# One token tile's down projection moved into the last twelve attention periods, and the first token sums loaded one at a time

## The chip, the cores and the metric

The kernel runs on one core of a Trainium2 chip. The metric is the device time of one execution in microseconds (us). Five engines work side by side, each through its own instructions in order: PE (matrix products), DVE (vector), ACT (activations), POOL (GpSimd) and SP, which here only issues DMA transfers; a transfer waits in SP's queue behind those issued ahead of it.

## The reference

32 heads of full attention (head width 16) beside a gated MLP, mixed by one gate per token; S = 2048 tokens, D = 512, F = 1792, all in fp32:

```python
def _A_ref(x, wqkv, wo):
    qkv = transpose((x @ wqkv).reshape(B, S, 3, H, Dh), 2, 0, 3, 1, 4)
    q, k, v = qkv[0], qkv[1], qkv[2]
    scores = einsum("bhqd,bhkd->bhqk", q, k) * Dh ** -0.5
    o = einsum("bhqk,bhkd->bhqd", softmax(scores), v)
    return transpose(o, 0, 2, 1, 3).reshape(B, S, D) @ wo

def _B_ref(x, w_gate, w_up, w_down):
    h = sigmoid(x @ w_gate) * (x @ w_up)
    return h @ w_down

g = sigmoid((x * gate_w).sum(-1, keepdims=True))
return g * _A_ref(x, wqkv, wo) + (1 - g) * _B_ref(x, w_gate, w_up, w_down)
```

## The kernel before

Every fp32 product is done as three products of operands split into a high and a low part (high by high, high by low, low by high); `split_weights` makes the two parts, by a cast and a subtraction.

After a start stage (values, first projections) come 256 *periods* (`NPER`), k = 0 to 255, and then an end stage. A period takes two steps of the attention: 8 score products (lines 574; "t" in the order strings) whose exponentials ACT computes (line 576), 8 products for row maxima (line 284, "m") that DVE reduces (line 286), and 32 small value products (line 715, `values(k)`). The maxima of a set are transposed and sent by SP through the DMA queue into rows of the query tile (`qs<-mt`, line 314) before the scores of that set are formed. Into every period 12 *half products* ("d0" on partitions 0 to 63, "d1" on 64 to 127) are woven, all into one bank of PSUM, `dn`. They come from a generator, `filling()`: first the projections of later heads' queries and keys (class `Sum`: both halves of a product add up in one bank; a run takes two periods), then the gate and up projections (class `Side`), for which sums and differences of token blocks ("token sums", `xm`) and of weights are formed on POOL. Two products on different halves of the partitions run side by side on PE; two on the same half one after another. Where both halves add up in one bank, PE may change halves only after an instruction of POOL that does nothing (`turn`), which waits for the last product and for which the next one waits.

PE's order in a period is a string written by hand (`STEADY`, and `LAST` for k = 248 to 255, where no row maxima are left). POOL's work is kept in a list, `later`, of which up to five pieces are run per period. The order of each engine's instructions is that in which the code issues them; the order of SP's queue is set by a scheduler. The gate and up results go to `gu_d` in DRAM. The token sums go to `xm_d` (line 335) and come back as tiles of four loads each (`mixed`, line 355).

The half-product work ends at k = 243. In periods 244 to 247 the strings still hold 12 slots, which stay empty. The first two weight tiles of the down projection, `wd0` and `wd1`, are split by POOL about k = 244; the others are loaded in pairs (`late_raw`, `late_next`), the first pair split at k = 252.

The end stage goes through 28 chunks, (c, f): c is a group of four token tiles, f a pair of rows of `w_down`. The hidden values of a chunk are loaded (`hidden_load`), gated by ACT and DVE and split (`hidden`, `hidden_split`); then come 6 products (line 919) for each of the four token tiles, into four banks. Between the chunks stand the heads' output products (`heads_out`, line 137): 8 pieces of 24 products. In all there are 672 down products and 192 of the heads.

Of the kernel before, what the change touches and what calls it, by code (L numbers as in the profile page):

```python
# [40 lines left out]
UPPER = FIRST + 4  # L41
EARLY = NPER - TAIL - 4
LOW, UP = 0, 1
MIX = ((((0, 0), "+", (1, 1)), ((0, 0), None, None)), (((0, 1), "-", (1, 1)), ((1, 0), "-", (0, 0))),
       (((0, 0), "+", (0, 1)), ((1, 0), "+", (1, 1))), (((1, 1), None, None), ((1, 1), None, None)))
BLOCKS = (((0, 0), (1, 0)), ((1, 1), (1, 1)), ((0, 0), (1, 1)), ((1, 0), (0, 1)), ((0, 0), (0, 0)), ((0, 1), (0, 1)))
# [3 lines left out]
def gated_mix(ctx, tc, x, xc, xmix, wqk, wv, wo, w_gu, w_down, gate_w, out):  # L50
# [25 lines left out]
    gu_d = dram.tile([2, NF, P, S], F32, name="gu_d")  # L76
    pv_d = dram.tile([NC, NPAIR, P, 256], F32, name="pv_d")
    rec_d = dram.tile([P, 512], F32, name="rec_d")

    warm = keep.tile([P, 96], F32, name="warm")  # L80
    dve.memset(warm, 0.0)
# [19 lines left out]
        lo.tensor_tensor(l, src, h.bitcast(F32), ALU.subtract)  # L101

    def raw_weights(src, shape, name, queue=sp):
        raw = keep.tile(shape, F32, name=name + "r", tag="wr", bufs=4)
        queue.dma_start(raw, src)
        return raw, shape, name

# [2 lines left out]

    def split_weights(loaded, *engines):
        raw, shape, name = loaded
        h = keep.tile(shape, F32R, name=name + "h", tag="wh", bufs=4)
        l = keep.tile(shape, F32R, name=name + "l", tag="wl", bufs=4)
# [44 lines left out]
    class Side:  # L159
# [12 lines left out]

        def done(self):
            return self.n == len(self.ops)

    def turn(*runs):

# [179 lines left out]

    parts = []

    def take(n):  # L360
        while parts and n:
            parts.pop(0)()
            n -= 1

    def mixtures():
        for cp in range(2):
            for fp in range(NF // 2):
                for a in range(2):
                    name = f"{cp}_{fp}_{a}"

                    def raw(n, rows=slice(0, P)):
                        t = keep.tile([P, 512], F32, name=f"r{n}_{name}", tag="wr", bufs=4)
                        sp.dma_start(t[rows, :], w_gu[a, fp, n, rows, :])
                        return t

                    def ready(n, x, y=None, op=None, rows=slice(0, P)):
                        h = keep.tile([P, 512], F32R, name=f"mh{n}_{name}", tag="wh", bufs=4)
                        l = keep.tile([P, 512], F32R, name=f"ml{n}_{name}", tag="wl", bufs=4)
# [49 lines left out]
        return arrive  # L428

    wd = []  # L430

    def filling():
        jobs = [(n, cp) for cp in range(2) for n in range(1, D // P)]
# [18 lines left out]
        for j, (n, cp) in enumerate(jobs):  # L452
            settle([raw for raw, _, _ in coming])
            ws, nxt = nxt, []
            for c in range(2):
                for i, w in enumerate(ws):
                    run = Sum(bankd(), unit(w, 2 * cp + c))
                    yield run
                    runs += 1
                    e = keep.tile([P, 512], F32R, name=f"qk{n}_{cp}_{c}_{i}", tag="er", bufs=6)  # L460
                    leave(e.bitcast(F32), run.o)
                    put_qk(e, (q_d, k_d)[i], n, 2 * cp + c)
                    next(mix, None)
# [12 lines left out]
        t = 0  # L476
# [1 line left out]
        for cp in range(2):  # L478
            for fp in range(NF // 2):
                for a in range(2):  # L480
                    arrive = combine(cp, fp, a)
                    order = [(j, g) for j in range(3) for g in ((LOW, UP) if a else (UP, LOW))] + [(3, LOW if a else UP)]
                    ws = []
                    for q, (j, g) in enumerate(order):
                        if len(ws) <= j:
                            ws.append(W.pop(0))
                        run = Side(bankd(), g, ws[j], T[j])
                        yield run
                        m = ((2, 1), (4, 3), (7, 6), (5, 5))[j][g]
# [12 lines left out]
                        take(1 if late_t and q < 4 and not cp else 2)  # L502
                if cp == 0 and fp == NF // 2 - 1:
                    late_t[3] = mixed(1, 3)
                    T = late_t
        arrived.pop(0)()
        wd.extend(split_weights(raw_weights(w_down[f * P:(f + 1) * P, :], [P, D], f"wd{f}")) for f in range(2))

    leave = lambda e, o: act.activation(e, o, AF.Copy)  # L509
    fill = filling()  # L510
# [116 lines left out]
    def down_late(f, raw, hi):  # L627
        if f < 6:
            for a in range(2):
                if f < 4:  # L630
                    h = keep.tile([P, D], F32R, name=f"wd{f + a}h", tag="wh", bufs=4)
                    l = keep.tile([P, D], F32R, name=f"wd{f + a}l", tag="wl", bufs=4)
                else:
                    h, l = wd45[:, a, 0, :], wd45[:, a, 1, :]
                split(h, l, raw[:, a, :], hi, pool)
                wd.append((h, l))
        else:
# [22 lines left out]
    def early_hidden(m, a):  # L660
        gu = loaded[m]
        dve.scalar_tensor_tensor(gu[:, 1, a], gu[:, 0, a], 1.0, gu[:, 1, a], op0=ALU.add, op1=ALU.mult)
        if a == 0:
            ready.append([[], []])
        h, l = [keep.tile([P, 512], F32R, name=f"h{i}_{m}_{a}", tag=("er", "wr")[m], bufs=(6, 4)[m]) for i in range(2)]
        split(h, l, gu[:, 1, a], dve, pool)
        ready[m][0].append(h)
        ready[m][1].append(l)
# [120 lines left out]
    stages = [[], []]  # L789
    for k in range(NPER):  # L790
        n = 2 * k
        if n + FIRST == NSTEP:
# [21 lines left out]
            pass  # L814
        elif run.done():
            run = next(fill, None)
        else:
            turn(run)
        work(3 if isinstance(run, Sum) and k % 2 else 4)
        urgent.extend(jobs)  # L820
        if 320 <= n < 448:
# [57 lines left out]
        split(oh, ol, ot, act, pool)  # L879
        return oh, ol  # L880

    bankt = turns([dn] + maxb)
    bankh = turns(banks)
    acc = {}

    def finish(t, o, gate):

# [4 lines left out]
        if (t, 0) in acc:  # L892
# [15 lines left out]
    heads = {}  # L908
    for n, (c, f) in enumerate(chunks):
        if f == 0:  # L910
            down = [bankt() for _ in range(4)]
# [71 lines left out]
```

## Time and profile before

| | us |
|---|---|
| time, median of three runs | 1692.49 (1691.63 to 1693.6) |
| the profiled execution, its own time | 1691.6 |
| its span, first to last instruction | 1689.8 |
| PE busy | 1681.1 |
| DVE busy | 1431.6 |
| ACT busy | 1335.4 |
| POOL busy | 1017.9 |

The profiled execution is 0.9 us faster than the median. Times in the rows of the profile count from the first instruction. A period of the loop is 5.52 us; the last value products of the periods start at 1489.27, and the end stage runs from there to the end. The granted TensorE clock is 0.999 on average.

### The profile page before, as it was taken

Reading aid. Unit: us, or ns where it says so; the run is one execution under the profiler, and the core shown is the slowest. Engines: PE = TensorE matmul, PEld = TensorE weight load, DVE = VectorE, ACT = ScalarE, POOL = GpSimd, SP = SyncE. Lnnn points to the kernel's source line nnn. Section 1 sums busy time; section 2 is a strip of 40 time slices with the busy share of each in tenths; the row PEclk is TensorE's granted clock in tenths of the full one; section 3 lists DMA queues with packets and bytes.
Section 4 is the critical chain, followed back from the end, with each engine's and each line's share of the span. In section 5 each row is a group of like instructions: output and inputs, shape, how many; then the busy total and the mean of one; then the engine's idle time right before and its main releaser. Section 6 shows DMA issues by size and latency. Waiting matters only on the chain.

```text
span 1689.8 us, 43420 instructions
## 1 busy us (share of the span) xinstructions
PE 1681.1 (99%) x16552; PEld 1153.2 (68%) x16552; DVE 1431.6 (85%) x2450; ACT 1335.4 (79%) x2668; POOL 1017.9 (60%) x1192
## 2 busy tenths in 40 slices
PE   9999999999999999999999999999999999999999
PEld 7866666666666666666666666666666666578887
DVE  6889989999999999999999999999999999567543
ACT  4188878888888888888888899999999988973321
POOL 1146655358878787776675777767777765452110
PEclk9999999999999999999999999999999999999999
DMA  9524675464444344442357242524242422176752
GB/s 259 116 83 167 181 250 144 125 162 135 127 136 139 120 145 126 120 121 79 89 154 209 84 114 80 130 71 120 83 116 78 107 83 95 61 266 224 243 194 72
DMA packets 125008, 228.54 MB, mean 135 GB/s; under 512 B 19008, under 2 KB 35648, under 8 KB 121792
## 3 DMA queue, kind: packets, MB, share of 16 engines
q1 hardware_dynamic: 124512, 225.24, 45.3%
q8 instruction: 131, 2.15, 0.6%
q14 instruction: 77, 0.63, 0.2%
q10 hardware_dynamic: 288, 0.52, 0.1%
HBM read 149.42 MB, written 75.76 MB: 133 GB/s over the span
## 4 chain that ended last, share of the span: by engine, by line
PE 98%; DMA 1%; ACT 1%; DVE 1%; SPq 0%; issue 0%; POOL 0%; ACTq 0%
PE dn L170 23%; PE sm L715 21%; PE sm L284 9%; PE st L284 9%; PE st L715 7%; PE sm L919 7%; PE dn L150 6%; PE sm L574 4%; PE st L137 4%; PE st L574 3%; PE dn L919 2%; PE st L150 1%; ACT p L576 0%; DMA xm<-xm_d 0%; DVE stat L286 0%; PE st L85 0%
## 5 line engine op out<-in xcount | busy, mean ns | idle before, releaser
L286 DVE TENSOR_REDUCE stat<-sm 128x1 f32<-128x512 f32 x1124 | 728.1, 682 | 77.3 <-PE sm L284 39.1
L576 ACT ACTIVATE p<-sm 128x512 f32<-128x512 f32 x1217 | 686.7, 630 | 7.5 <-PE sm L574 5.3
L286 DVE TENSOR_REDUCE stat<-st 128x1 f32<-128x512 f32 x924 | 606.7, 682 | 64.2 <-PE sm L574 27.0
L576 ACT ACTIVATE p<-st 128x512 f32<-128x512 f32 x831 | 499.6, 634 | 5.5 <-PE st L574 4.1
L170 PE MATMUL dn<-xm,mh 64*128 64x512 f32 x1568 | 485.6, 389 | 0.0
L574 PE MATMUL sm<-qs,ks 64*128 64x512 f32 x1217 | 445.5, 404 | 0.3 <-ACT p L576 0.2
L284 PE MATMUL sm<-ks,qs 48*128 48x512 f32 x1124 | 421.6, 421 | 0.4 <-ACT p L576 0.3
L284 PE MATMUL st<-ks,qs 48*128 48x512 f32 x924 | 367.9, 426 | 0.0
L715 PE MATMUL sm<-p,v 128*17 128x256 f32 x6080 | 365.1, 380 | 0.1
L574 PE MATMUL st<-qs,ks 64*128 64x512 f32 x831 | 325.7, 409 | 3.0 <-DMA qs<-mt 3.0
L170 PEld LDWEIGHTS dn<-xm,mh 64*128 64x128 f32 x1568 | 289.6, 185 | 29.7
L170 PE MATMUL dn<-xm,ml 64*128 64x512 f32 x784 | 304.0, 388 | 0.0
L715 PEld LDWEIGHTS sm<-p,v 128*17 128x17 f32 x6080 | 160.3, 97 | 169.4 <-ACT p L576 58.4
L284 PEld LDWEIGHTS sm<-ks,qs 48*128 48x128 f32 x1124 | 200.4, 185 | 87.6 <-DVE stat L286 76.5
L574 PEld LDWEIGHTS sm<-qs,ks 64*128 64x128 f32 x1217 | 219.1, 186 | 18.4 <-ACT p L576 3.1
L284 PEld LDWEIGHTS st<-ks,qs 48*128 48x128 f32 x924 | 167.0, 185 | 83.9 <-DVE stat L286 75.5
L733 POOL TENSOR_TENSOR sum<-sum,part 128x256 f32<-128x256 f32 x192 | 141.7, 738 | 86.9 <-ACT part L720 63.4
L407 POOL TENSOR_TENSOR m<-m,m 128x512 f32<-128x512 f32 x140 | 178.2, 1289 | 5.7 <-ACT m L509 5.7
L574 PEld LDWEIGHTS st<-qs,ks 64*128 64x128 f32 x831 | 152.7, 186 | 16.2 <-issue 4.6
L100 POOL CAST mxs<-mxs 128x4 fp32r<-128x4 f32 x128 | 24.1, 188 | 219.6 <-DVE mxs L298 219.3
L170 PEld LDWEIGHTS dn<-xm,ml 64*128 64x128 f32 x784 | 144.4, 184 | 11.8
L123 POOL TENSOR_TENSOR ml<-r,mh 128x512 fp32r<-128x512 f32 x112 | 144.0, 1286 | 7.0
(225 smaller groups left out, 2288.4 us busy)
## 6 DMA issues: line engine op xcount, KB each, us to landing
r<-in_w_gu_dram SPq DMA_DIRECT2D x112, 256.0 KB
gul<-gu_d SPq DMA_DIRECT2D x56, 512.0 KB
gu_d<-m SPq DMA_DIRECT2D x84, 256.0 KB
xm_d<-xm SPq DMA_DIRECT2D x32, 512.0 KB
xm<-xm_d SPq DMA_DIRECT2D x32, 512.0 KB
xm<-in_xmix_dram SPq DMA_DIRECT2D x24, 512.0 KB
qs<-q_d SPq DMA_DIRECT2D x90, 128.0 KB
ks<-k_d SPq DMA_DIRECT2D x90, 128.0 KB
```

The lines of the kernel that those rows point to most:

```text
L123: pool.tensor_tensor(l, src, h.bitcast(F32), ALU.subtract)
L137: pe.matmul(o, a, b, start=(i == 0), stop=(i == len(ops) - 1))
L150: mm = pe.matmul(self.o, a[rows], b[rows], start=(self.n == 0), stop=(self.n == 2 * len(self.ops) - 1))
L170: pe.matmul(self.o, a, b, start=(self.n == 0), stop=(self.n == len(self.ops) - 1))
L284: pe.matmul(t, qs[r:r + KM, qt * P:(qt + 1) * P], ks[r:r + KM, g * 512:(g + 1) * 512], start=True, stop=True)
L286: dve.tensor_reduce(stat[part][:, qt % 4, g:g + 1], t, axis=AX.X, op=ALU.max)
L407: pool.tensor_tensor(o, x, y, op)
L574: pe.matmul(o, ks[r:r + KR, (kt + a) * P:(kt + a + 1) * P], qs[r:r + KR, c * 512:(c + 1) * 512], start=True, stop=True)
L576: act.activation(pt[:, a, :], o, AF.Exp, scale=DH ** -0.5)
L715: pe.matmul(o[r:r + VW, :], v[:, 4 * k % 16 + a, h * VW:(h + 1) * VW], pts[b][:, a, 256 * i:256 * i + 256], start=(a == 0), stop=(a == 3))
L733: pool.tensor_tensor(s, s, e, ALU.add)
L919: pe.matmul(down[t], a, b, start=(f == 0 and m == 0), stop=(f == NF - 2 and m == 5))
```

## The change

Token tile 4 (`AHEAD`) leaves the end stage: its 42 products (14 rows of `w_down`, three each) are done as 84 half products, in the bank `dn`, in periods 244 to 255. Periods 244 to 247 take 12 each into slots that were empty; 248 to 251 take 18 upper halves and 252 to 255 18 lower halves, as the strings say. For this the hidden values of tile 4 are formed at k = 152 to 164 in four pieces (ACT, POOL, by `h_d` in DRAM), loaded again about k = 239 into a buffer of the token tiles, and all 14 tiles of `w_down` are loaded and split by POOL from k = 239 on; `wd0` to `wd3` stay for the end stage, the others are loaded a second time there, as before. The split weights have six buffers in place of four. The end stage makes 630 down products; the result of tile 4 is scaled out of `dn` by DVE at the fifth chunk and added with the heads.

The loads of the first two token sums are begun earlier (after runs 12 and 16, not 14 and 17), and each waits for ACT's copy of the run after which it is issued.

```diff
+    class Down(Sum):
+        def __init__(self):
+            self.o, self.n, self.last, self.token = dn, 0, None, None
+            self.ops, self.left = range(6 * NF // 2), [[], []]
+        def give(self, h, w):
+            for side in self.left:
+                side += terms([(h, w)])
...
-    def take(n):
+    def take(n, behind=None):
         while parts and n:
-            parts.pop(0)()
+            load = parts.pop(0)()
+            if behind:
+                tc.add_manual_dep(load.ins, behind.ins.name, SYNC, reason="one at a time")
             n -= 1
...
+    def hidden_ahead(g):
+        fs = slice(4 * g, min(4 * g + 4, NF))
+        n = (fs.stop - fs.start) * P
+        e = keep.tile([P, 2, 512], F32R, name=f"ha{g}", tag="ev", bufs=2)
+        f = e.bitcast(F32)
+        for a in range(2):
+            sp.dma_start(f[:, a, :n].rearrange("p (f s) -> p f s", s=P),
+                         gu_d[a, fs, :, AHEAD * P:(AHEAD + 1) * P].rearrange("f p s -> p f s"))
+        yield
+        act.activation(f[:, 0, :n], f[:, 0, :n], AF.Tanh, scale=0.5)
+        def store():
+            pool.tensor_tensor(e[:, 1, :n], f[:, 1, :n], f[:, 0, :n], ALU.subtract)
+            sp.dma_start(h_d[:, :, fs, :], f[:, :, :n].rearrange("p i (f s) -> p i f s", s=P))
+        later.append(lambda: pool.tensor_tensor(f[:, 0, :n], f[:, 0, :n], f[:, 1, :n], ALU.mult))
+        later.append(lambda: pool.tensor_tensor(f[:, 1, :n], f[:, 0, :n], f[:, 1, :n], ALU.add))
+        later.append(lambda: pool.tensor_copy(e[:, 0, :n], f[:, 1, :n]))
+        later.append(store)
+        yield
...
+    def weights_ahead():
+        i = len(raw_ahead) - 2
+        f = order_ahead[i]
+        w = split_weights(raw_ahead[i])
+        raw_ahead.append(raw_down(order_ahead[i + 2]) if i + 2 < NF else None)
+        down_ahead.give((held[0][:, 0, f, :], held[0][:, 1, f, :]), w)
+        if f < 4:
+            wd.append(w)
...
-                    leave(e.bitcast(F32), run.o)
+                    left = leave(e.bitcast(F32), run.o)
...
-                    if runs in (14, 17, 22, 24):
+                    if runs in (12, 16, 22, 24):
                         T[len(T)] = mixed(0, len(T))
-                    take(2 if runs > 21 else 1)
+                    take(2 if runs > 21 else 1, left if runs < 21 else None)
...
-    late = [(w_down, f, down_late) for f in range(2, NF, 2)] + [(wo, k, heads_weights) for k in range(0, KT, 2)]
+    late = [(w_down, f, down_late) for f in range(4, NF, 2)] + [(wo, k, heads_weights) for k in range(0, KT, 2)]
...
-    LAST = ["t0 t0 t0 work t0 t1 t1 t1 t1"] * TAIL
+    LAST = ["t0 d1 t0 d1 t0 d1 t0 d1 d1 work t1 t1 t1 t1", "t0 d1 t0 d1 t0 d1 t0 d1 work t1 t1 t1 t1"] * 2 + [
+        "t0 t0 t0 t0 work t1 d0 t1 d0 t1 d0 t1 d0 d0", "t0 t0 t0 t0 work t1 d0 t1 d0 t1 d0 t1 d0"] * 2
...
-        else:
+        elif k < NPER - TAIL or k == NPER - TAIL + 3:
             turn(run)
+        if EARLY <= k < EARLY + 6:
+            for _ in range(2 if k < EARLY + 3 else 1):
+                weights_ahead()
+        if n in (304, 308, 312, 316):
+            ahead_h.append(hidden_ahead((n - 304) // 4))
+            next(ahead_h[-1])
+        if n in (308, 312, 316, 320):
+            next(ahead_h[(n - 308) // 4])
...
-        if n == NSTEP - 8:
-            late_next(dve)
...
         for t in range(4):
+            if 4 * c + t == AHEAD:
+                continue
```

SP's queue where the token sums come back: `xm<-xm_d` is such a load, `xm_d<-xm` the store of a token block, `xm<-in_xmix_dram` the load of the next block, `q_d` and `k_d` the stores of a finished projection, `qs<-mt` the row maxima. Before (line 355 is the load):

```order
119 L238 DMA k_d<-qh_1_2810 128x512
120 L238 DMA k_d<-qk_0_1_1_2808 128x512
121 L314 DMA qs_102<-mt_3_1_2805 2x4x32 x4
122 L735 DMA pv_d<-sum_1_2597 128x256
123 L355 DMA xm_0_3126<-xm_d 128x2x512
124 L355 DMA xm_1_3603<-xm_d 128x2x512 x2
125 L335 DMA xm_d<-xm_2_2_2737 256x1x512
126 L355 DMA xm_1_3603<-xm_d 128x2x512 x2
127 L325 DMA xm_3_0_3051<-in_xmix_dram 128x512
128 L238 DMA q_d<-qh_2_2965 128x512
129 L238 DMA q_d<-qk_1_0_0_2963 128x512
130 L314 DMA qs_102<-mt_3_0_2960 2x4x32 x4
```

After, between the same sets of maxima and the next (line 369 is the load):

```order
122 L328 DMA qs_103<-mt_3_1_2806 2x4x32 x4
123 L795 DMA pv_d<-sum_1_2598 128x256
124 L349 DMA xm_d<-xm_2_2_2738 256x1x512
125 L339 DMA xm_3_0_3055<-in_xmix_dram 128x512
126 L369 DMA xm_0_2812<-xm_d 128x2x512
127 L252 DMA q_d<-qh_2_2968 128x512
128 L252 DMA q_d<-qk_1_0_0_2966 128x512
129 L328 DMA qs_103<-mt_3_0_2963 2x4x32 x4
130 L349 DMA xm_d<-xm_2_3_2897 256x1x512
131 L339 DMA xm_3_1_3212<-in_xmix_dram 128x512
132 L369 DMA xm_0_2812<-xm_d 128x2x512
```

Five loads stood between two sets of `qs<-mt`; now there is one, and it stands behind the store and the load of the next block.

PE in a period of the tail, the scores of `st` and `sm` banks between two groups of value products. Before:

```order
9294 L574 MATMUL st_65<-qs_102,ks_103 128x512
9295 L574 MATMUL sm_69<-qs_102,ks_103 128x512
9296 L574 MATMUL sm_70<-qs_102,ks_103 128x512
9297 L574 MATMUL st_67<-qs_102,ks_103 128x512
9298 L574 MATMUL sm_71<-qs_102,ks_103 128x512
9299 L574 MATMUL st_66<-qs_102,ks_103 128x512
9300 L574 MATMUL sm_72<-qs_102,ks_103 128x512
9301 L574 MATMUL st_65<-qs_102,ks_103 128x512
```

After (line 152 is a half product of `hh`, the hidden values of tile 4):

```order
9356 L638 MATMUL st_65<-qs_103,ks_104 128x512
9357 L152 MATMUL dn<-wd2h,hh 128x512
9358 L638 MATMUL sm_69<-qs_103,ks_104 128x512
9359 L152 MATMUL dn<-wd3h,hh 128x512
9360 L638 MATMUL sm_70<-qs_103,ks_104 128x512
9361 L152 MATMUL dn<-wd3l,hh 128x512
9362 L638 MATMUL st_67<-qs_103,ks_104 128x512
9363 L152 MATMUL dn<-wd3h,hh 128x512
9364 L638 MATMUL sm_71<-qs_103,ks_104 128x512
9365 L638 MATMUL st_66<-qs_103,ks_104 128x512
9366 L638 MATMUL sm_72<-qs_103,ks_104 128x512
9367 L638 MATMUL st_65<-qs_103,ks_104 128x512
```

Four upper halves now stand between the four scores on lower rows; the four scores on upper rows follow alone.

SP's queue about k = 158 to 160: `gu_d<-m` stores gate and up results, `r<-in_w_gu_dram` loads weights. Before:

```order
522 L373 DMA r_1_1_0_13402<-in_w_gu_dram 128x512
523 L314 DMA qs_102<-mt_3_0_13159 2x4x32 x4
524 L373 DMA r_1_1_0_13404<-in_w_gu_dram 128x512
525 L373 DMA r_1_1_0_13480<-in_w_gu_dram 128x512
526 L373 DMA r_1_1_0_13633<-in_w_gu_dram 128x512
527 L314 DMA qs_100<-mt_0_1_13316 2x4x32 x4
528 L735 DMA pv_d<-sum_2_13111 128x256
529 L409 DMA gu_d<-m_1_0_1_13162 128x512
530 L373 DMA r_1_1_0_13720<-in_w_gu_dram 64x512
531 L373 DMA r_1_1_0_13722<-in_w_gu_dram 64x512
532 L314 DMA qs_100<-mt_0_0_13473 2x4x32 x4
```

After (`ha` is a piece of tile 4's hidden values):

```order
525 L389 DMA r_1_1_0_13660<-in_w_gu_dram 128x512
526 L462 DMA h_d<-ha_13093 256x1x512
527 L389 DMA r_1_1_0_13749<-in_w_gu_dram 64x512
528 L455 DMA ha_13418<-gu_d 128x4x128 x2
529 L328 DMA qs_101<-mt_0_1_13327 2x4x32 x4
530 L795 DMA pv_d<-sum_2_13115 128x256
531 L425 DMA gu_d<-m_1_0_1_13166 128x512
532 L389 DMA r_1_1_0_13751<-in_w_gu_dram 64x512
533 L462 DMA h_d<-ha_13254 256x1x512
534 L389 DMA r_1_1_1_13991<-in_w_gu_dram 128x512
535 L455 DMA ha_13580<-gu_d 128x2x128 x2
536 L328 DMA qs_101<-mt_0_0_13492 2x4x32 x4
```

A store of one piece and the loads of the piece after the next now stand ahead of each set of `qs<-mt`; those loads go into the buffer that the store reads.

More of the change, by code (lines that the diff above doesn't have):

```diff
@@ L43 @@
 LOW, UP = 0, 1
+AHEAD = 4
 MIX = ((((0, 0), "+", (1, 1)), ((0, 0), None, None)), (((0, 1), "-", (1, 1)), ((1, 0), "-", (0, 0))),
@@ L78, in gated_mix @@
     rec_d = dram.tile([P, 512], F32, name="rec_d")
+    h_d = dram.tile([P, 2, NF, P], F32, name="h_d")
     warm = keep.tile([P, 96], F32, name="warm")
@@ L103, in raw_weights @@
     def raw_weights(src, shape, name, queue=sp):
-        raw = keep.tile(shape, F32, name=name + "r", tag="wr", bufs=4)
+        raw = keep.tile(shape, F32, name=name + "r", tag="wr", bufs=6)
         queue.dma_start(raw, src)
@@ L112, in split_weights @@
         raw, shape, name = loaded
-        h = keep.tile(shape, F32R, name=name + "h", tag="wh", bufs=4)
-        l = keep.tile(shape, F32R, name=name + "l", tag="wl", bufs=4)
+        h = keep.tile(shape, F32R, name=name + "h", tag="wh", bufs=6)
+        l = keep.tile(shape, F32R, name=name + "l", tag="wl", bufs=6)
         if engines:
@@ L174, in done @@
             return self.n == len(self.ops)
+    class Down(Sum):
[5 more added lines that the diff above has]
+                side += terms([(h, w)])
+    down_ahead = Down()
     def turn(*runs):
@@ L371, in raw @@
                     def raw(n, rows=slice(0, P)):
-                        t = keep.tile([P, 512], F32, name=f"r{n}_{name}", tag="wr", bufs=4)
+                        t = keep.tile([P, 512], F32, name=f"r{n}_{name}", tag="wr", bufs=6)
                         sp.dma_start(t[rows, :], w_gu[a, fp, n, rows, :])
@@ L376, in ready @@
                     def ready(n, x, y=None, op=None, rows=slice(0, P)):
-                        h = keep.tile([P, 512], F32R, name=f"mh{n}_{name}", tag="wh", bufs=4)
-                        l = keep.tile([P, 512], F32R, name=f"ml{n}_{name}", tag="wl", bufs=4)
+                        h = keep.tile([P, 512], F32R, name=f"mh{n}_{name}", tag="wh", bufs=6)
+                        l = keep.tile([P, 512], F32R, name=f"ml{n}_{name}", tag="wl", bufs=6)
                         if op:
@@ L430, in gated_mix, with load_ahead, raw_down @@
     wd = []
+    held = []
+    def hidden_ahead(g):
[16 more added lines that the diff above has]
+        yield
+    order_ahead = [*range(4, NF), *range(4)]
+    raw_ahead = []
+    def load_ahead():
+        held.append(xp.tile([P, 2, KT, 512], F32R, name="hh", tag="xt", bufs=4).rearrange(
+            "p i k s -> p i (k s)")[:, :, :NF * P].rearrange("p i (f s) -> p i f s", s=P))
+        for i in range(2):
+            sp.dma_start(held[0][:, i].bitcast(F32), h_d[:, i])
+        raw_ahead.extend(raw_down(f) for f in order_ahead[:2])
+    def raw_down(f):
+        return raw_weights(w_down[f * P:(f + 1) * P, :], [P, D], f"wd{f}")
+    def weights_ahead():
[6 more added lines that the diff above has]
+            wd.append(w)
     def filling():
@@ L502, in filling @@
                         take(1 if late_t and q < 4 and not cp else 2)
+                        if cp and fp == NF // 2 - 1 and a:
+                            if q == 1:
+                                load_ahead()
+                            elif q > 1:
+                                weights_ahead()
                 if cp == 0 and fp == NF // 2 - 1:
@@ L506, in filling @@
         arrived.pop(0)()
-        wd.extend(split_weights(raw_weights(w_down[f * P:(f + 1) * P, :], [P, D], f"wd{f}")) for f in range(2))
+        yield down_ahead
     leave = lambda e, o: act.activation(e, o, AF.Copy)
@@ L629, in down_late @@
             for a in range(2):
-                if f < 4:
-                    h = keep.tile([P, D], F32R, name=f"wd{f + a}h", tag="wh", bufs=4)
-                    l = keep.tile([P, D], F32R, name=f"wd{f + a}l", tag="wl", bufs=4)
-                else:
-                    h, l = wd45[:, a, 0, :], wd45[:, a, 1, :]
+                h, l = wd45[:, a, 0, :], wd45[:, a, 1, :]
                 split(h, l, raw[:, a, :], hi, pool)
@@ L664, in early_hidden @@
             ready.append([[], []])
-        h, l = [keep.tile([P, 512], F32R, name=f"h{i}_{m}_{a}", tag=("er", "wr")[m], bufs=(6, 4)[m]) for i in range(2)]
+        h, l = [keep.tile([P, 512], F32R, name=f"h{i}_{m}_{a}", tag=("er", "wr")[m], bufs=6) for i in range(2)]
         split(h, l, gu[:, 1, a], dve, pool)
@@ L789, in gated_mix @@
     stages = [[], []]
+    ahead_h = []
     for k in range(NPER):
@@ L816, in gated_mix @@
             run = next(fill, None)
-        else:
+        elif k < NPER - TAIL or k == NPER - TAIL + 3:
             turn(run)
+        if EARLY <= k < EARLY + 6:
+            for _ in range(2 if k < EARLY + 3 else 1):
+                weights_ahead()
+        if n in (304, 308, 312, 316):
[3 more added lines that the diff above has]
+            next(ahead_h[(n - 308) // 4])
         work(3 if isinstance(run, Sum) and k % 2 else 4)
@@ L880, in heads_split @@
         return oh, ol
-    bankt = turns([dn] + maxb)
-    bankh = turns(banks)
+    bankt = turns([dn] + maxb[2:] + maxb[:2])
+    bankh = turns(banks[1:] + banks[:1])
     acc = {}
+    ahead = lp.tile([P, D], F32, name="ahead")
     def finish(t, o, gate):
@@ L891, in finish @@
         a = acc[c][:, t % 4, :]
-        if (t, 0) in acc:
+        if t == AHEAD:
+            dve.scalar_tensor_tensor(a, o, gate[:, t:t + 1], ahead, op0=ALU.mult, op1=ALU.add)
+            sp.dma_start(out[t * P:(t + 1) * P, :], a)
+        elif (t, 0) in acc:
             dve.scalar_tensor_tensor(a, o, gate[:, t:t + 1], a, op0=ALU.mult, op1=ALU.add)
@@ L910, in gated_mix @@
         if f == 0:
-            down = [bankt() for _ in range(4)]
+            down = [bankt() if 4 * c + t != AHEAD else None for t in range(4)] if c else [maxb[3], banks[0], maxb[0], maxb[1]]
+        if n == 4:
+            g = g0[:, AHEAD:AHEAD + 1]
+            dve.tensor_scalar(ahead, dn, g, None, op0=ALU.mult)
         if n in at:
```

## The prediction

> **What bounds the kernel now.** I read the busy table of the page first, then the chain that ended last, then PE's timeline period by period, and last the waits of the place where a period is too long.
>
> ```profile
> PE 1681.1 (99%) x16552; PEld 1153.2 (68%) x16552; DVE 1431.6 (85%) x2450; ACT 1335.4 (79%) x2668; POOL 1017.9 (60%) x1192
> PE 98%; DMA 1%; ACT 1%; DVE 1%; SPq 0%; issue 0%; POOL 0%; ACTq 0%
> L574 PE MATMUL st<-qs,ks 64*128 64x512 f32 x831 | 325.7, 409 | 3.0 <-DMA qs<-mt 3.0
> L286 DVE TENSOR_REDUCE stat<-sm 128x1 f32<-128x512 f32 x1124 | 728.1, 682 | 77.3 <-PE sm L284 39.1
> ```
>
> PE carries the chain, so the sum below is a sum over PE: products that leave a stretch where PE never waits shorten it by their pitch, and products that enter one cost their pitch unless another engine paces it. The second row leaves 2% to others. The third (score products; last the idle time ahead of them) names a wait of 3.0 us on a DMA, and by the timeline it is a single one.
>
> ```profile
> 238.70 1.06 PE L715 MATMUL sm<-p,v 128*17 128x256 f32 x16
> 244.09 0.46 PE L574 MATMUL st<-qs,ks 64*128 64x512 f32 x1 [3.04 <-DMA qs<-mt]
> 249.06 0.63 PE L715 MATMUL sm<-p,v 128*17 128x256 f32 x8
> ...
> 966.62 1.92 PE L715 MATMUL sm<-p,v 128*17 128x256 f32 x32
> 972.14 1.92 PE L715 MATMUL sm<-p,v 128*17 128x256 f32 x32
> 1452.08 1.92 PE L715 MATMUL sm<-p,v 128*17 128x256 f32 x32
> 1457.60 1.92 PE L715 MATMUL st<-p,v 128*17 128x256 f32 x32
> 1461.18 1.92 PE L715 MATMUL sm<-p,v 128*17 128x256 f32 x32
> 1484.70 1.92 PE L715 MATMUL st<-p,v 128*17 128x256 f32 x32
> 1489.27 1.92 PE L715 MATMUL st<-p,v 128*17 128x256 f32 x32
> ...
> 244.20:248.20 4.00, 4.00 (x22) 3.77 (x24) 1.98 (x3) 2.93 (x6) 0.00 (x0) 0.57 0.61 203
> ```
>
> The value matmuls (L715) open each period, so the distance between two such rows is a period. In the loop it is 972.14 − 966.62 = 5.52 us; here it is 249.06 − 238.70 = 10.36, a loss of 4.84: 3.04 of waiting, and some 1.8 because the clock granted afterwards is 0.57 (the third number from the right of the window row) for four microseconds. [...]
>
> From 1461.18 to 1484.70 six periods take 23.52, that is 3.92 each (k=248 to 253, where no row-max product runs). The last, to 1489.27, takes 4.57.
>
> **First part of the change: the first token sums.** Why is `qs<-mt` late at 241?
>
> ```profile
> 213.31 0.62 SPq L355 DMA_DIRECT2D xm<-xm_d  x1
> 214.67 1.75 SPq L355 DMA_DIRECT2D xm<-xm_d  x2
> 227.38 1.89 SPq L355 DMA_DIRECT2D xm<-xm_d  x3
> 229.38 0.57 SPq L335 DMA_DIRECT2D xm_d<-xm  x1
> 229.99 2.27 SPq L355 DMA_DIRECT2D xm<-xm_d  x2
> 238.34 0.34 SPq L325 DMA_DIRECT2D xm<-in_xmix_dram  x1
> 239.73 2.77 SPq L314 DMA_DIRECT2D qs<-mt  x4
> ...
> SPq L325 <- DMA xm_d<-xm: 13.0, 3, 6.0
> 241.88 2.08 DMA qs<-mt
> ```
>
> Eight loads of 512 KB leave within 19 us. The store at 229.38 shares the DMA engines with five of them; the load at 238.34, which reuses the stored buffer, waits 6.0 for it (longest number of the wait row), and the row maxima behind it in SP's queue leave at 239.73. The order of SP's rows after the change has one such load between two sets of `qs<-mt`, tied to ACT's copy of that run, which the store of the same run awaits anyway. So store and load take turns and the long wait has no cause: −4.84. Against it stands a floor of 0, if the load behind the store alone sufficed. All 831 score products of that row together waited 3.0 for `qs<-mt`, so nowhere else did a store and a load alone make the maxima late: I take the full value.
>
> **Second part: 42 products leave the end stage.**
>
> ```profile
> 1530.03 0.39 PE L919 MATMUL dn<-wd1h,hl 128*128 128x512 f32 x1
> 1537.96 0.39 PE L919 MATMUL sm<-wd2h,hl 128*128 128x512 f32 x1
> 1491.00:1686.00 195.00, 194.91 (x862) 160.96 (x858) 116.72 (x96) 66.08 (x67) 42.19 (x17) 1.00 0.60 201
> ```
>
> The first two rows are 35 products apart: 7.93 / 35 = 0.2266 us each. PE is busy 194.91 of 195.00 there, so nothing else sets the pace: 42 × 0.2266 = −9.52, if the operands come that much earlier. The chunks with token tile 4 shrink by six products (1.36) each, seven times.
>
> **Third part: the same products as 84 halves in periods 244 to 255.** 48 of them fill k=244 to 247, whose slots are empty now, yet those periods last 5.52 (rows 1452.08 and 1457.60): eight maxima on DVE at 0.682 (row L286) are 5.46 of it, and the loop's full periods last the same 5.52. So 48 halves cost 0; if that cover were gone, at most 0.23 each, 11. The other 36 go into k=248 to 255, where a slot's price is the difference of the two kinds of period: by PE's order 14 serial slots in the loop, 7 in the tail (products on different halves of the rows run side by side, those on the same half one after another), (5.52 − 3.92) / 7 = 0.229. The last period confirms it: three slots more, 4.57 − 3.92 = 0.65. After the change, halves on one half of the rows run beside scores on the other; counted along PE's order by the slot rule above, four periods have 9 serial slots and four 8. That is 3.92 + 2 × 0.229 = 4.38 and 4.15. But ACT paces the tail too:
>
> ```profile
> 1461.00:1489.00 28.00, 28.00 (x283) 14.64 (x282) 11.07 (x19) 28.00 (x59) 11.24 (x11) 1.00 0.41 128
> ```
>
> ACT (fourth busy number) is busy 28.00 of 28.00, so a period cannot fall below 3.92; but it gets no work from the halves and is no bound above 3.92, so PE's slots count: four times 0.46, three times 0.23, and for the last period four slots, 0.92: 1.84 + 0.69 + 0.92 = +3.45. Ends: 0.92, if ACT alone set the pace before the last period, and 36 × 0.229 = 8.2, if no half found a partner. I keep 3.4, near the slot count, since PE's order fixes the pairs.
>
> **What this needs, and what hides it.** Hidden values of token tile 4 are computed at k=152 to 164: four tanh on ACT (each inside the 1.2 of 11 us in which ACT idles, below), 16 POOL operations, four stores, eight loads. The 14 weight tiles need 14 casts and 14 subtractions on POOL, of which two pairs stood there before.
>
> ```profile
> L123 POOL TENSOR_TENSOR ml<-r,mh 128x512 fp32r<-128x512 f32 x112 | 144.0, 1286 | 7.0
> L127 POOL CAST mh<-r 128x512 fp32r<-128x512 f32 x112 | 68.5, 612 | 5.0
> 954.00:965.00 11.00, 11.00 (x124) 7.23 (x122) 9.99 (x19) 9.75 (x22) 8.16 (x10) 1.00 0.24 79
> 1424.00:1446.00 22.00, 22.00 (x218) 14.18 (x216) 19.96 (x37) 19.51 (x41) 11.53 (x15) 1.00 0.18 62
> 963.10 1.43 SPq L314 DMA_DIRECT2D qs<-mt  x2
> 974.00 0.49 PE L574 MATMUL st<-qs,ks 64*128 64x512 f32 x1
> ```
>
> The fifth busy number of a window is POOL's. In 1424 to 1446 it is 11.53 of 22, so with the two old pairs (3.8) taken out some 14 us are free there, and 5 more to 1451, where the last of wd4 to wd11 is wanted: 19 against 8 × 1.90 = 15.2. They fit, with little over; the DMA engines are busy 0.18 there, so the weights and the 1.8 MB of hidden values land. Cost 0, with POOL's lateness as a rival.
>
> At k=152 to 164 a piece adds 3 × 1.29 + 0.61 = 4.48 to every two periods, and the window holds 8.16 of 11 already. Laid one after another on POOL's rows, its work runs up to 5 late, which PE does not see directly, since gate and up weights are split two units ahead. But in SP's order the store of a piece and the loads of the next now stand ahead of a `qs<-mt` set. That set leaves at 963.10 now and is read at 974.00; from the first issue to the landing it is 4.2 (rows 239.73 and 241.88 + 2.08). With POOL's lateness and the landing of one small store I estimate the departure 5.4 later, at 968.5: landed near 972.7, 1.3 early. Cost 0, ends 0 and +4.84 (another wait as at 241).
>
> **What is given back in the end stage.** Chunk 8 and the first heads will be wanted 1.36 and 2.72 earlier.
>
> ```profile
> 1529.99 1.22 DVE L101 TENSOR_TENSOR hl<-gul,hl 128x1024 fp32r<-128x1024 f32 x1
> 1533.52 2.41 POOL L101 TENSOR_TENSOR ol<-ot,oh 128x1024 fp32r<-128x1024 f32 x1 [8.54 <-ACT oh L98]
> 1533.43 0.39 PE L919 MATMUL sm<-wd2h,hl 128*128 128x512 f32 x1
> 1538.87 0.62 PE L137 MATMUL st<-weights,oh 128*128 128x512 f32 x2
> ```
>
> Chunk 8: ready 1531.2, wanted 1533.43 − 1.36 = 1532.07. Heads: `ol` ready 1535.93, wanted by their third product, 1538.87 + 2 × 0.23 − 2.72 = 1536.6. Both hold by under 1 us; later needs move earlier by up to 9.5 but have more room. The loads for the first heads now wait until PE has read the hidden values, and stand in the busiest DMA stretch. I put +0.7 there, as if one of the two were missed by as much as it holds by, between 0 and 3 (a 2.4 us POOL step and a little more).
>
> ```profile
> 1505.98 3.42 DVE L101 TENSOR_TENSOR hl<-gul,hl 128x1024 fp32r<-128x1024 f32 x1
> 1505.17 3.15 POOL L101 TENSOR_TENSOR wd_l<-late,wd_h 128x1024 fp32r<-128x1024 f32 x1 [0.19 <-ACT wd_h L98]
> ```
>
> The same DVE operation that takes 1.22 at 1529.99, with POOL idle, takes 3.42 at 1505.98 beside POOL, whose step takes 3.15. The new POOL work of the tail (wd1 to wd3 last) stands beside DVE's gating of the first hidden values, which is of this kind. I keep 0, since these weights are wanted some periods after their split; the other end is a rival. [...]
>
> **Sum.** −4.84 − 9.52 + 3.4 + 0.7 = −10.3. The profiled execution took 1691.6, 0.9 below the median shown, so 1681.3 there and 1682.2 as a median.
>
> **Rivals.**
> *Supply bounds the end stage.* If operands come no earlier, the saving of 9.52 shrinks; losing half, 1687.0, losing all, 1691. For: margins under 1 us. Against: they are at the start only. Chance 0.10, half of it above 1689.
> *A new wait for `qs<-mt` near k=160.* +4.84 at most: 1687.0. For: the margin of 1.3 us rests on an estimated backlog. Chance 0.15.
> *The spacing does not remove the old wait* (the change does not do what it says): 1687.0, chance 0.05.
> *POOL and DVE hold each other up in the tail.* If each of the last three weights is late by one POOL step of 1.29, PE waits up to 3.9: 1686.1, chance 0.04. [...]
> *No half finds a partner:* 8.2 in place of 3.4, 1687.0, chance 0.04.
> *Slower:* POOL does not finish the split weights. POOL's tokens that let PE change rows stand in the same queue, so PE waits in each of k=245 to 251. It decides when POOL falls behind by 10.3 + 3.4 = 13.7 us, some 2 per period, to 1696; by the prices above that needs each of 28 operations to take half as long again. Chance 0.04.
>
> **Numbers.** The likeliest case, 0.58, has its own range 1680 to 1684.5 (tail +1.5 to +4, give-back 0 to 2). With the rivals at 1687 the range is 1679.6 to 1687.5; about 0.12 lies outside. A measurement here tells about 0.2%, 3.4 us, from no change: faster 0.88 (all cases but half of the first rival, some sums of two, and the slower one), same 0.08, slower 0.04.
>
> **What would show it.** No PE wait for `qs<-mt` near 240 and a period of 5.5 there; none at 974; periods of about 4.4 and 4.15 in the tail; the end stage 9.5 shorter from the first product after the last values to the end, without PE waits. Wrong: a PE wait above 1 us at k=244 to 252 on POOL, tail periods above 4.9, or PE waits for `hl` or `ol`.

## The result, and the profile after

The changed kernel takes 1683.53 us (median of 4 runs, 1682.06 to 1685.74) beside 1693.05 for the kernel before in the same session: ratio 0.995, 95% interval 0.9937 to 0.9964. The profiled execution took 1682.67 with a span of 1680.9, against 1691.6 and 1689.8. So 8.9 us of span are gone, and 9.5 by the medians; 10.3 were forecast (1682.2 as a median).

Where they went, by the starts of the value products (L715 before, L775 after) and the ends of the spans:

| stretch | forecast, us | measured, us |
|---|---|---|
| start stage, to the first period | 0 | −0.4 (89.55 to 89.16; the other kernels below start between 88.75 and 90.02, so none of it can be put down to the change) |
| the wait near 240 | −4.84 | −4.85 |
| periods 244 to 255 | +3.4 | +1.97 |
| end stage | −9.52 + 0.7 = −8.8 | −5.66 |

The stall is gone. PE's timeline and SP's queue of the changed kernel, at the place of the wait, and the group of score products whose idle time was 3.0:

```profile
238.29 1.92 PE L775 MATMUL sm<-p,v 128*17 128x256 f32 x32
243.80 1.06 PE L775 MATMUL sm<-p,v 128*17 128x256 f32 x16
...
219.30 0.61 SPq L369 DMA_DIRECT2D xm<-xm_d  x1
225.25 0.58 SPq L349 DMA_DIRECT2D xm_d<-xm  x1
228.28 0.34 SPq L339 DMA_DIRECT2D xm<-in_xmix_dram  x1
228.72 0.60 SPq L369 DMA_DIRECT2D xm<-xm_d  x1
231.17 2.72 SPq L328 DMA_DIRECT2D qs<-mt  x4
...
L638 PE MATMUL st<-qs,ks 64*128 64x512 f32 x831 | 324.8, 408 | 0.0
```

The store leaves at 225.25 and the load behind it at 228.28: 2.5 us of waiting in place of 6.0, and the maxima are on their way at 231.17. The period is 243.80 − 238.29 = 5.51.

The tail of the changed kernel, the same rows as before:

```profile
1452.39 1.92 PE L775 MATMUL st<-p,v 128*17 128x256 f32 x32
1456.52 1.92 PE L775 MATMUL sm<-p,v 128*17 128x256 f32 x32
1460.41 1.92 PE L775 MATMUL sm<-p,v 128*17 128x256 f32 x32
1464.54 1.92 PE L775 MATMUL sm<-p,v 128*17 128x256 f32 x32
1480.56 1.92 PE L775 MATMUL st<-p,v 128*17 128x256 f32 x32
1486.03 1.92 PE L775 MATMUL st<-p,v 128*17 128x256 f32 x32
```

Periods with five halves last 4.13, those with four 3.89, less than the 3.92 of before without any half; the last lasts 5.47.

The end stage is the surprise. PE now waits twice, and the rows of DVE and SP before it show for what:

```profile
1572.80 0.50 PE L996 MATMUL sm<-wd0h,hl 128*128 128x512 f32 x1 [2.55 <-DVE hl L103]
1576.12 0.50 PE L996 MATMUL dn<-wd0h,hl 128*128 128x512 f32 x1 [0.76 <-DVE acc L965]
...
1570.39 1.23 DVE L734 SCALAR_TENSOR_TENSOR gul<-gul 128x1024 f32<-128x1024 f32 x1 [9.18 <-DMA gul<-gu_d]
1571.53 1.22 DVE L103 TENSOR_TENSOR hl<-gul,hl 128x1024 fp32r<-128x1024 f32 x1
...
1550.35 2.46 SPq L683 DMA_DIRECT2D gul<-gu_d  x3
1555.43 1.23 SPq L940 DMA_DIRECT2D rb<-rec_d  x2
1559.02 1.83 SPq L939 DMA_DIRECT2D ot<-pv_d  x3
1563.73 3.71 SPq L683 DMA_DIRECT2D gul<-gu_d  x5
...
1556.58 2.41 POOL L103 TENSOR_TENSOR ol<-ot,oh 128x1024 fp32r<-128x1024 f32 x1 [11.57 <-DMA gul<-gu_d]
```

Read from the top: PE wants the low part of the hidden values (`hl`) of chunk 14, counted from 0: (c, f) = (2, 0). DVE makes it at 1571.53, but in DVE's order the gating of chunk 15 (L734) comes first, and that waits 9.18 us for a load. The two chunks need four loads (`gul`). Three leave at 1550.35; the fourth stands in SP's queue behind the eight loads of the fourth heads piece (`rb`, `ot`), whose buffers POOL frees at 1559 (1556.58 + 2.41), and leaves at 1563.73, the first of the five in that row. Before the change all four stood ahead of the heads' loads; the low part of chunk 14 was ready at 1568.59 and first read, by the chunk's third product, at 1582.84:

```profile
1552.67 0.46 SPq L619 DMA_DIRECT2D gul<-gu_d  x1
1554.07 2.79 SPq L619 DMA_DIRECT2D gul<-gu_d  x3
1558.66 2.48 SPq L872 DMA_DIRECT2D rb<-rec_d  x4
...
1567.36 1.23 DVE L101 TENSOR_TENSOR hl<-gul,hl 128x1024 fp32r<-128x1024 f32 x1 [0.91 <-ACT hl L98]
1582.84 0.39 PE L919 MATMUL sm<-wd0h,hl 128*128 128x512 f32 x1
```

### The profile page after: what moved, and what is told of

Same layout as the page of the kernel before. It is cut to its first block, busy times and chain, and to the rows that moved or that the text cites. A ratio compares the mean times of both kernels' runs of the same rounds, so it can differ in the third digit from the quotient of the medians.

```text
span 1680.9 us, 43590 instructions
## 1 busy us (share of the span) xinstructions
PE 1672.5 (100%) x16594; PEld 1148.6 (68%) x16594; DVE 1430.3 (85%) x2448; ACT 1337.7 (80%) x2672; POOL 1051.9 (63%) x1230
## 4 chain that ended last, share of the span: by engine, by line
PE 94%; DMA 3%; DVE 1%; POOL 1%; SPq 0%; issue 0%; ACT 0%; DVEq 0%; ACTq 0%
PE dn L172 23%; PE sm L775 22%; PE sm L298 10%; PE st L298 9%; PE st L775 7%; PE dn L152 7%; PE sm L638 4%; PE sm L996 3%; PE st L638 3%; PE st L139 3%; PE st L152 1%; DMA gul<-gu_d 1%; PE dn L996 1%; DMA den<-pv_d 1%; DMA ot<-pv_d 0%; DMA late<-in_w_down_dram 0%
## 5 line engine op out<-in xcount | busy, mean ns | idle before, releaser
L775 PE MATMUL sm<-p,v 128*17 128x256 f32 x6080 | 365.1, 380 | 0.1
L775 PEld LDWEIGHTS sm<-p,v 128*17 128x17 f32 x6080 | 160.3, 97 | 169.5 <-ACT p L640 58.5
```

The lines of the kernel that those rows point to most:

```text
L775: pe.matmul(o[r:r + VW, :], v[:, 4 * k % 16 + a, h * VW:(h + 1) * VW], pts[b][:, a, 256 * i:256 * i + 256], start=(a == 0), stop=(a == 3))
```

## Experiments

**The first token sums.** Three kernels take the small part of the change alone, on the kernel before: both edits, the dependency without the earlier start, the earlier start without the dependency.

```diff
-            parts.pop(0)()
+            load = parts.pop(0)()
+            if behind:
+                tc.add_manual_dep(load.ins, behind.ins.name, SYNC, reason="one at a time")
...
-                    if runs in (14, 17, 22, 24):
+                    if runs in (12, 16, 22, 24):
```

space_only, both:

> The kernel before with the first token sums changed alone: begun after runs 12 and 16, each load tied to ACT's copy of its run. The down projection is as before. Theory A (the eight bunched loads delayed the store, so the load behind it and with it the row maxima): no PE wait for qs<-mt near 240, that period 5.5 in place of 10.4, the whole 4.8 to 5.3 us shorter, about 1687.5. Rival (the maxima are late because of the load behind the store alone): a wait of about 3 stays near 240 and the time stays within 1 us of 1692.5.

Measured: 1688.34 us, ratio 0.9976 (0.9966 to 0.9986). In the profile the wait is gone, the period is 5.52, and the span 4.8 shorter (1685.0). Theory A holds. By the medians only 3.5 us are gained; the profiled execution (1686.76) is among the fastest of runs that go from 1686.63 to 1689.42.

dependency_only, the first part of the diff, with ACT's copy handed to `take` as in the change:

> The kernel before with the dependency alone: each load of the first two token sums waits for ACT's copy of its run; the sums are begun after runs 14 and 17 as before. SP's order then has one such load per two periods, ending one set of maxima later than in the change. Theory A (the bunch is what delays the store): the wait near 240 is gone, 4.8 us off as with both parts. Rival F (the earlier start is what matters, since it leaves two more sets of room): a wait remains, here or a few periods later, and less than 2 us are gained.

Measured: 1687.64, ratio 0.9966 (0.9953 to 0.9979), span 1685.1. SP's queue and its longest waits (last number) between 200 and 250:

```profile
SPq L325 <- DMA xm_d<-xm: 7.4, 3, 2.7
231.88 2.67 SPq L314 DMA_DIRECT2D qs<-mt  x4
```

No PE wait for `qs<-mt` is left. In this kernel the first load of a token sum leaves only at 240.04, so none stands near the store at all.

early_start_only, the last line alone:

> The kernel before with the first token sums begun after runs 12 and 16, without the dependency. SP's order still bunches the loads, four before and four between two sets of maxima. Theory A: a period of 10 to 13 us near 240 stays, the time is within 3 us of before. Rival F: the wait is gone and 4.8 us are gained.

Measured: 1691.59, ratio 0.9996 (0.9986 to 1.0005). In the profile the wait is smaller but there, and the period lasts 246.94 − 237.93 = 9.01; SP's wait, PE's, and two windows of 2 us:

```profile
SPq L325 <- DMA xm_d<-xm: 11.7, 3, 5.2
241.97 0.47 PE L574 MATMUL st<-qs,ks 64*128 64x512 f32 x1 [1.69 <-DMA qs<-mt]
242.00:244.00 2.00, 2.00 (x14) 1.86 (x16) 1.06 (x2) 1.53 (x3) 0.94 (x3) 0.74 0.69 265
244.00:246.00 2.00, 2.00 (x13) 1.80 (x11) 0.92 (x2) 1.56 (x5) 0.00 (x0) 0.50 0.45 116
```

The period is shorter than the 10 to 13 that theory A expected, but the wait stays. So it is the dependency that helps, since it breaks the bunch: the load behind the store waits for it 6.0 at the longest with the bunch, 5.2 with the bunch and the earlier start, 2.9 in space_only and in the changed kernel, where one load leaves per period, and 2.7 with none near it. Rival F falls.

**The down projection alone**, with the token sums loaded as before (the lines above taken back in the changed kernel):

> The changed kernel with the first token sums loaded as before (eight in a bunch); the down projection of token tile 4 stays moved. Theory A: the wait near 240 is back (10.4 us period) and the rest is as in the changed kernel: tail +2.0, end stage 5.7 shorter, so 3.7 below before, about 1688.8, and with the run above the two parts add up to the whole change within 1 us. Rival (the parts need each other, for instance because the earlier token sums free SP's queue later on): the sum of the two savings misses the 9 us of both together by 2 or more.

Measured: 1691.24, ratio 0.9993 (0.9984 to 1.0002): no difference that can be told, where 3.7 us were expected. The two parts alone sum to about 4 us (3.5 and 0.6), the change gives 9. Its profile (span 1690.8) shows where the rest went: the waits of PE, and windows behind them with the granted clock third from the right.

```profile
246.11 0.76 PE L636 MATMUL st<-qs,ks 64*128 64x512 f32 x1 [4.72 <-DMA qs<-mt]
1582.44 0.79 PE L994 MATMUL sm<-wd0h,hl 128*128 128x512 f32 x1 [4.29 <-DVE hl L103]
...
246.00:250.00 4.00, 3.89 (x18) 3.39 (x20) 1.98 (x3) 2.22 (x5) 0.00 (x0) 0.50 0.54 173
1582.00:1587.00 5.00, 4.56 (x14) 3.71 (x15) 4.89 (x8) 3.44 (x4) 2.31 (x1) 0.66 0.34 116
```

The bunch falls a little differently in SP's queue and costs more (the period lasts 12.61, 2.25 more than before), and the wait in the end stage is 4.29 here, with a low clock behind it, so that the end stage gains 3.7 in place of 5.7. The tail costs the same 1.98. So the sum misses the whole by some 5 us, as the rival said, and in the profiles most of the difference lies in two waits: the one near 240 is larger than in the kernel before, the one in the end stage larger than in the changed kernel. Whether the spacing of the token sums makes the second wait smaller, and how large it is in executions without a profile, is not shown.

**The load in the end stage.** Each load of hidden values is issued one chunk earlier in the code, in the changed kernel:

```diff
-    loaded.extend(hidden_load(*chunks[m]) for m in range(2, 4))
+    loaded.extend(hidden_load(*chunks[m]) for m in range(2, 5))
...
-        if n + 4 < len(chunks):
-            loaded.append(hidden_load(*chunks[n + 4]))
+        if n + 5 < len(chunks):
+            loaded.append(hidden_load(*chunks[n + 5]))
```

> The changed kernel with each load of hidden values of the end stage issued one chunk earlier in the code (five chunks ahead in place of four), which puts both loads of the chunk after the seventh of group 1's successor ahead of the heads' loads in SP's queue; nothing else moves. Theory B (3.3 us of PE waiting at 1572 and 1576 come from one load of 512 KB that stands in SP's queue behind eight loads for the heads, which wait for POOL): the PE wait for hl goes, the end stage is 2.5 to 3.5 us shorter, about 1680, and runs scatter less. Rival C (the DMA engines are at their limit there, so the load lands late wherever it stands): the wait stays above 1.5 us and the time within 1 us of the changed kernel.

Measured: 1679.15 us, all of its runs between 1678.94 and 1679.74; ratio 0.9921 (0.9907 to 0.9934). Here the fourth load leaves ahead of the heads' loads, and DVE goes on without a wait:

```profile
1552.28 1.24 SPq L683 DMA_DIRECT2D gul<-gu_d  x2
1558.82 0.60 SPq L939 DMA_DIRECT2D ot<-pv_d  x1
...
1560.93 1.21 DVE L734 SCALAR_TENSOR_TENSOR gul<-gul 128x1024 f32<-128x1024 f32 x1
1562.07 1.21 DVE L103 TENSOR_TENSOR hl<-gul,hl 128x1024 fp32r<-128x1024 f32 x1
...
1560.00:1580.00 20.00, 20.00 (x90) 16.49 (x89) 13.19 (x14) 8.60 (x9) 2.41 (x1) 1.00 0.82 282
```

The low part of chunk 14 is ready at 1563.3 in place of 1572.75, and PE is busy 20.00 of 20.00. From the last value products (1486.53) to the end of the span (1677.5) it is 190.97, against 200.53 before: 9.56 less, the 42 products at 0.2266 and nothing lost; against the changed kernel (194.87) it is 3.90 less, a little more than expected. Rival C falls: the DMA engines move 282 GB/s in that window and the load is in time; its place in the queue was wrong. The edit moves every load of the end stage, not this one alone; both PE waits are gone with it.

The same edit on the kernel before:

> The kernel before with each load of hidden values issued one chunk earlier in the code, nothing else. If the loads of the end stage limit only because the moved tile takes the slack (theory B), this is worth nothing here: PE has no wait in the end stage before, and the time is within 0.5 us of it. Rival: the earlier loads help for another reason (DVE and POOL less often side by side, less contention) and 1 us or more is gained here too.

Measured: 1692.43, ratio 0.9995 (0.9986 to 1.0004), no PE wait in the end stage of its profile, as in the kernel before. So the earlier loads are no gain by themselves. Whether the order of the changed kernel would have cost anything without the moved tile is not shown, since in the kernel before the four loads already stood ahead of the heads'.

**The tail.** The 36 halves as 6, 3, 6, 3 per period:

```diff
-    LAST = ["t0 d1 t0 d1 t0 d1 t0 d1 d1 work t1 t1 t1 t1", "t0 d1 t0 d1 t0 d1 t0 d1 work t1 t1 t1 t1"] * 2 + [
+    LAST = ["t0 d1 t0 d1 t0 d1 t0 d1 d1 d1 work t1 t1 t1 t1", "t0 d1 t0 d1 t0 d1 t0 work t1 t1 t1 t1"] * 2 + [
```

(and the lower halves likewise)

> The changed kernel with the 36 tail halves as 6, 3, 6, 3 per period in place of 5, 4, 5, 4. Theory D (a period costs what its serial slots on PE cost, 0.24 each above 8 slots, and never less than ACT's pace of 3.9): periods with 6 last 4.35 to 4.4, those with 3 still 3.9, the tail about 0.9 longer in all. Rival E (each half costs 0.24 wherever it stands): periods with 6 last 4.37, those with 3 last 3.65, the tail unchanged.

Measured: 1685.49 in one run, span 1683.7. The value products:

```profile
1453.10 1.92 PE L775 MATMUL st<-p,v 128*17 128x256 f32 x32
1457.44 1.92 PE L775 MATMUL sm<-p,v 128*17 128x256 f32 x32
1461.11 1.92 PE L775 MATMUL sm<-p,v 128*17 128x256 f32 x32
1465.45 1.92 PE L775 MATMUL sm<-p,v 128*17 128x256 f32 x32
```

4.34, 3.67, 4.34: theory D falls and rival E holds. With the 3.89 and 4.13 of the changed kernel, 3, 4, 5 and 6 halves give 3.67, 3.89, 4.13 and 4.34, nearly a straight line, of about 0.22 a half. From the last loop period to the last value products it takes 33.63 here and 33.64 in the changed kernel: the distribution is worth nothing. And 3.92 is no floor of a single period, but ACT's pace over several: in the changed kernel's 33.64 us ACT is busy 32.71, and with periods of 4.34 and 3.67 in turn the stretch is no longer (33.63).

The last kernel uses this: 24 halves in the tail, which ACT's pace covers, and the six products left over whole, after the last scores, on top of the earlier loads (the lines replaced, the earlier loads and one more `turn`, in period 254, are left out here):

```diff
+    LAST = ["t0 d1 t0 d1 t0 d1 t0 work t1 t1 t1 t1"] * 4 + [
+        "t0 t0 t0 t0 work t1 d0 t1 d0 t1 d0 t1 d0"] * 3 + ["t0 t0 t0 work t0 t1 t1 t1 t1"]
...
+    for i, (a, b) in enumerate(down_ahead.left[LOW]):
+        mm = pe.matmul(dn, a, b, start=False, stop=(i == len(down_ahead.left[LOW]) - 1))
```

> The changed kernel with the hidden values loaded one chunk earlier, and 24 tail halves in place of 36 (3 per period, then 4, none in the last); the six products left over are done whole, in the same bank, after the last scores. Theory G (PE's price of a half is 0.23 to 0.24, but the tail is paced by ACT at 3.92 a period up to some 4 halves, and only what lies above is paid): the tail grows by at most 0.4 over before in place of 2.0, the end stage is 36 x 0.2266 = 8.2 shorter in place of 9.5, together 0.3 to 0.5 below the run with the earlier loads alone, near 1678.8. Rival: the tail's cost comes from something else than the count of halves (the change of rows, the wait for POOL), and the tail still costs 1.5 or more: 1680 or above.

Measured: 1678.87 (1678.44 to 1679.83), ratio 0.9912 (0.9897 to 0.9927). The first two periods, with three halves, last 3.66 and 3.83; from the third on, periods with three and with four halves both come to ACT's 3.92, as in these rows:

```profile
1464.92 1.92 PE L775 MATMUL sm<-p,v 128*17 128x256 f32 x32
1468.85 1.92 PE L775 MATMUL sm<-p,v 128*17 128x256 f32 x32
1472.77 1.92 PE L775 MATMUL st<-p,v 128*17 128x256 f32 x32
```

From period 247 to 254 it takes 27.09, against 27.10 before: the 24 halves cost nothing. Without its start stage, which took 0.5 longer in this profile, it is 0.5 below the run with the earlier loads alone (1677.5 − 90.02 = 1587.5 against 1677.5 − 89.51 = 1588.0), as expected; in whole times the two can't be told apart. Both beat the changed kernel: 14.0 and 12.7 us below the kernel before, in place of 9.5, each against the runs of before in its own session.

## Why the prediction was right, and where not

The sum was close (10.3 forecast, 8.9 of span measured) because errors had opposite signs: the end stage gave 3.2 less than forecast, the tail cost 1.4 less, and the start stage was 0.4 shorter, which the change does not explain. That they cancel in part is luck.

*The wait near 240.* Right in size (4.84 and 4.85; the 1.8 of low clock went with the wait, since the period is 5.51 and the granted clock 1.00 from 238 to 250) and in cause; dependency_only and early_start_only show that breaking the bunch suffices and that starting earlier does not. The floor of 0 and the rival that the spacing would not remove the wait fall with it.

*42 products at 0.2266.* Right: with the load in its place the end stage loses 9.56.

*The tail, +3.4.* Mis-sized by 1.4: 1.97 measured, in periods of 4.13 and 3.89 where 4.38 and 4.15 were forecast. The price of a half, 0.229, came out right (about 0.22), and so did the last period's 0.92 (5.47 − 4.57 = 0.90). In part that is luck, since the price was taken from 5.52 − 3.92 over seven slots, and 3.92 was ACT's: with three halves, which by the same rule leave seven slots, PE needs 3.67, and (5.52 − 3.67) / 7 would have been 0.264. Wrong was the step that put the slots on top of 3.92 as if PE had set that pace: it was ACT's. On the line above, four halves need 3.89 on PE, so about four halves a period were free, and only the fifth cost 0.24. The step said that ACT "is no bound above 3.92", which is true, and missed that below 3.92 PE had room.

*The give-back in the end stage, +0.7.* This is the step that failed: "later needs move earlier by up to 9.5 but have more room". The first two needs, each forecast with under 1 us of margin, both held. The wait came at chunk 14, the first after the seven shortened chunks, where PE's demand has moved furthest: 3.86 were given back (9.52 − 5.66), above the range of 0 to 3, and of it 2.55 and 0.76 are the two waits; no row names the other 0.55. PE waits for `hl`, one of the signs that the prediction gave for being wrong.

The demand alone would not have done it. Before, chunk 14 was read 14.25 after it was ready (1582.84 − 1568.59), and 9.52 off that still leaves 4.7. What failed is that the forecast kept the supply's times of the kernel before: one load of 512 KB changed its place in SP's queue against eight others, and `hl` of chunk 14 was ready 86.72 after the end stage began (1572.75 − 1486.03) in place of 79.32 (1568.59 − 1489.27), 7.4 later. Why the scheduler placed the load there is not shown. The rival "supply bounds the end stage" named the right stage but the wrong limit: it is a queue's order, not the rate.

*A new wait near k=160* did not come. In the changed kernel, with POOL's window (fifth busy number) and SP's queue:

```profile
944.00:955.00 11.00, 11.00 (x123) 7.23 (x122) 9.99 (x19) 10.26 (x22) 10.79 (x14) 1.00 0.36 121
959.30 0.58 SPq L462 DMA_DIRECT2D h_d<-ha  x1
963.31 2.72 SPq L328 DMA_DIRECT2D qs<-mt  x4
```

All times are 5.2 earlier here, so the forecast departure, 968.5, is 963.3: it came at 963.31, closer than an estimated backlog can promise. POOL is busy 10.79 of 11. The margin is less sure than that: the next set leaves at 975.69, 6.8 later than before (974.13 − 5.2 = 968.9), which was not forecast, and PE does not wait for it either; how much room it had is not shown.

*POOL's late weights, and POOL against DVE in the tail*: PE waits nowhere in periods 244 to 255, so neither the slower rival nor that of POOL and DVE holding each other up took place; no run shows how near either was.

## What to carry to other kernels

When work leaves a stage that PE bounds, check the supply in the queue's new order and not by the old times, above all at the end of the shortened stretch, where the demand has moved furthest: one load behind a group that waits for a buffer can hold up two engines (here DVE for 9.18 us and PE for 2.55). Where two engines keep nearly the same pace, price added work from the engine that has to do it and count the room up to the other's pace as free (here PE needs 3.67 with three halves and ACT 3.92). Two savings measured alone need not add up to the change (here 3.5 and 0.6, and 9 together) when each leaves a wait whose size differs from one schedule to the next (near 240, a period of 10.36 before and of 12.61 in down_only).

## What the runs showed of the hardware

Half the clock follows some short waits and not others: after 1.69 us without a product (early_start_only) the granted clock falls to 0.50 (the window 244 to 246 above), about a microsecond after PE has begun again (241.97), and products come at 0.43 in place of 0.23 until 246; after the 2.55 of the changed kernel it stays at 1.00:

```profile
1573.00:1578.00 5.00, 4.24 (x18) 3.18 (x18) 4.89 (x7) 3.91 (x4) 2.39 (x1) 1.00 0.53 191
```

So the wait of 1.69 cost 3.49 (9.01 − 5.52), while the two waits of the changed kernel, 3.31 together, are nearly all of the 3.86 that its end stage gave back. What decides which wait the low clock follows is not shown.

The changed kernel scatters from 1682.06 to 1685.74 with mean clocks from 1.000 down to 0.997, hidden_load_early from 1678.94 to 1679.74, all at 1.000. That the clock behind the waits makes this scatter is not shown: only one execution of each kernel has a trace, and space_only and dependency_only, whose profiles lack the wait near 240, the only PE wait above 0.3 us that the kernel before has after its start stage, still go from 1686.63 to 1689.42 and from 1686.85 to 1689.08, with mean clocks down to 0.998.
